# Where operand tiles begin: w and o tiles at 128 mod 256 bytes, the other operand tiles at 0

## The chip, the cores and the metric

The kernel runs on one core of a Trainium2 chip. The metric is the device time of one execution in microseconds; the time before is the median of three runs. One further execution was recorded by the hardware profiler, and every row shown below comes from it.

## The reference: attention, a squared-ReLU MLP and four experts

```python
scores = q @ k.T / sqrt(64)            # 2 x 8 heads, 576 positions, 64 wide
attn = softmax(where(mask, scores, -1e9)) @ v   # heads 0-3: last 32 positions; 4-7: every 32nd
x = attn as (1152, 512)
x = relu(x @ w_in) ** 2 @ w_out        # w_in 512 x 2048, w_out 2048 x 512
p = domain_probs / (domain_probs.sum(-1) + 1e-9)
out = sum over e in 0..3 of p[:, e] * (relu(x @ w1[e]) @ w2[e])   # w1 512 x 1024, w2 1024 x 512
```

All of it is float32.

## The kernel before

A product in the MLP and the experts is made of three matmuls in TensorE's type fp32r. Each operand is kept as two halves, a rounded one ("hi") and what is left ("lo"), and `mm3` (L787 to L790) multiplies hi by hi, hi by lo and lo by hi into one PSUM tile. A matmul has a stationary operand (`lhsT`, 128 columns, brought in by a weight load that the trace shows as a row of its own, PEld) and a moving operand (`rhs`, 384 or 512 columns that stream past it).

Which tile is which operand:

- `x0` to `x2` (the activations, transposed, 384 tokens each), `h0` to `h3` (hidden values) and `t0` to `t2` (sums of activations for the fast matrix products of Strassen's kind) are moving operands of `mm3`. In the second product of an expert, in `second` (L1328 to L1330), hidden values in `h`, `x` or `t` tiles are the stationary operand.
- `w0` to `w9` hold weights that were split into hi and lo, the stationary operand of `mm3`. In the last stage some of them serve otherwise: the first 6144 bytes of such a tile hold sums of activations (moving) and the last 2048 bytes a left operand (stationary). The first two of the second expert weights (`std_w2`) also stand in a w tile, as the moving operand of L1328 to L1330.
- `o0` to `o2` hold all the other second expert weights, split, as the moving operand of L1328 to L1330.
- `q`, `k`, `v`, `p`, `pt` are the attention's, in plain float32; `raw`, `mid`, `val`, `r`, `sf`, `c0`, `acc`, `y0`, `y1` are read and written by DMAs, VectorE, ScalarE and GpSimd only.

The order of the work is written by a planner (`Plan`): every task has a cost, a rank and the tasks it comes after, and a simulation of engines and buffers fixes the order in which instructions are issued. It knows names, costs and free buffers, and no addresses. Attention runs in the first 90 us beside the first MLP products; the MLP follows, then the experts. While TensorE has nothing at the start, a filler (L1477) multiplies the bf16 tile `idle`.

Tiles are laid into SBUF in the order in which they are allocated, pool after pool: `const`, `main`, then `attn` and later `late` in the same place; `early` and later `last` stand at the other end and end at the same byte. The lines that matter:

```python
pe_s = const.tile([P, NT // P], F32, name="pe_s")
xt = many(main, "x", NB, [P, 2, KD, TB], F32R)
...
plan.ring("w", many(main, "w", NW, [P, 2, 4 * CH], F32R))
plan.ring("raw", many(main, "raw", NRAW, [P, 4 * CH], U32))
...
late["w2", k] = rp.tile([P, 2, DM], F32R, name=f"o{k}")
```

In the built program of before `x0` begins at byte 18336 of each partition, 160 mod 256, and since the tiles after it are multiples of 512 bytes long, `w`, `raw`, `mid`, `val`, `h`, `r`, `acc`, `t` and `sf` tiles begin at 160 mod 256 too. The `o` tiles begin at 217056, 221152 and 225248, which is 224 mod 256. The bf16 tile `idle` begins at 17856, 192 mod 256. Every operand of an fp32r matmul is a slice that begins a whole multiple of 512 bytes after its tile.

Of the kernel before, what the change touches and what calls it, by code (L numbers as in the profile page):

```python
# [7 lines left out]
F32 = mybir.dt.float32  # L8
# [8 lines left out]
P = 128  # L17
# [180 lines left out]
def tile_attention_mlp_experts(ctx: ExitStack, tc: tile.TileContext, a, out):  # L198
# [5 lines left out]
    const = ctx.enter_context(tc.tile_pool(name="const", bufs=1))  # L204
    main = ctx.enter_context(tc.tile_pool(name="main", bufs=1))
# [13 lines left out]
    def many(pool, name, n, shape, dtype=F32):  # L219
        return [pool.tile(shape, dtype, name=f"{name}{i}") for i in range(n)]  # L220
# [57 lines left out]
    idle = const.tile([P, P], BF16, name="idle")  # L278
    pe = const.tile([P, NT // P, E], F32, name="pe")
    pe_s = const.tile([P, NT // P], F32, name="pe_s")  # L280
    xt = many(main, "x", NB, [P, 2, KD, TB], F32R)
    spill = many(ep, "y", NB - 1, [P, KD, TB])
    plan.ring("w", many(main, "w", NW, [P, 2, 4 * CH], F32R))
    plan.ring("raw", many(main, "raw", NRAW, [P, 4 * CH], U32))
    plan.ring("mid", many(main, "mid", NMID, [P, 2 * CH]))
    plan.ring("val", many(main, "val", NMID, [P, 2 * CH]))
# [894 lines left out]
    def open_last(e):  # L1181
        early.close()
        rp = ctx.enter_context(tc.tile_pool(name="last", bufs=1, side="right"))
        for k in range(3):
            late["w2", k] = rp.tile([P, 2, DM], F32R, name=f"o{k}")

    t_last = plan.add({"none": 1}, open_last, after=t_sums, rank=0, adds=[("w2", [("w2", k) for k in range(3)]), ("tmp", [("tmp", 0)])])
    plan.add({"none": 1}, lambda e: None, after=[pair_end, t_late], rank=0, adds=[("hid", [("h", k) for k in range(hk)])])

# [377 lines left out]
```

## Time and profile before

| | |
|---|---|
| time, median of 3 runs | 615.72 us (615.61 to 615.83) |
| profiled execution, span from the first to the last instruction | 614.7 us |
| around the span (median less span) | 1.0 us |
| TensorE busy | 608.4 us, 99% of the span |
| VectorE, ScalarE, GpSimd busy | 452.9, 302.4, 125.4 us |
| moved by DMA | 45.14 MB |

Busy shares are of the span. A matmul's record reaches from its start to the modelled end of its drain, so that records of neighbouring matmuls overlap; what a matmul costs is the time from its start to the start of the next one. A row of the timeline that merges several instructions says how many (x6) and reaches from the start of the first to the end of the last.

### The profile page before, as it was taken

Reading aid. Unit: us, or ns where it says so; the run is one execution under the profiler, and the core shown is the slowest. Engines: PE = TensorE matmul, PEld = TensorE weight load, DVE = VectorE, ACT = ScalarE, POOL = GpSimd, SP = SyncE. Lnnn points to the kernel's source line nnn. Section 1 sums busy time; section 2 is a strip of 40 time slices with the busy share of each in tenths; the row PEclk is TensorE's granted clock in tenths of the full one; section 3 lists DMA queues with packets and bytes.
Section 4 is the critical chain, followed back from the end, with each engine's and each line's share of the span. In section 5 each row is a group of like instructions: output and inputs, shape, how many; then the busy total and the mean of one; then the engine's idle time right before and its main releaser. Section 6 shows DMA issues by size and latency. Waiting matters only on the chain.

```text
span 614.7 us, 10054 instructions
## 1 busy us (share of the span) xinstructions
PE 608.4 (99%) x3737; PEld 558.4 (91%) x3737; DVE 452.9 (74%) x900; ACT 302.4 (49%) x705; POOL 125.4 (20%) x150
## 2 busy tenths in 40 slices
PE   8999999999999999999999999999999999999997
PEld 5898999999999999998898989898998989898996
DVE  5997958774797984977666675858866776987654
ACT  3676875656464653665244534344344534344330
POOL 2421202310010101032031231312141322224000
PEclk9999999999999999999999999999999999999999
DMA  8987332131213100020110202020201203020012
GB/s 262 315 262 204 110 110 92 34 108 66 102 50 89 36 0 18 1 86 18 38 49 20 84 18 86 18 86 17 71 16 36 70 17 86 18 86 1 1 52 103
DMA packets 37441, 45.14 MB, mean 73 GB/s; under 512 B 4688, under 2 KB 26640, under 8 KB 37392
## 3 DMA queue, kind: packets, MB, share of 16 engines
q1 hardware_dynamic: 37392, 44.50, 23.7%
q8 instruction: 29, 0.48, 0.3%
q14 instruction: 20, 0.16, 0.1%
HBM read 42.13 MB, written 2.36 MB: 72 GB/s over the span
## 4 chain that ended last, share of the span: by engine, by line
PE 97%; DMA 1%; ACT 0%; DVE 0%; SPq 0%; issue 0%; POOL 0%; ACTq 0%
PE bh L788 12%; PE bh L790 12%; PE bh L789 12%; PE by L1329 11%; PE by L1328 11%; PE by L1330 11%; PE by L788 5%; PE by L790 5%; PE by L789 5%; PE ba L788 4%; PE ba L790 4%; PE ba L789 3%; PE ba L516 1%; PE ba L502 1%; DMA q<-in_ql_dram 1%; DMA k<-in_ks_dram 1%
## 5 line engine op out<-in xcount | busy, mean ns | idle before, releaser
L1281 DVE SCALAR_TENSOR_TENSOR acc<-by,pe,acc 128x512 f32<-128x512 f32 (+1 forms) x109 | 79.3, 743 | 24.2 <-PE by L1330 23.9
L788 PE MATMUL bh<-x,w 128*128 128x384 f32 x234 | 80.4, 344 | 0.0
L790 PE MATMUL bh<-x,w 128*128 128x384 f32 x234 | 78.4, 335 | 0.0
L789 PE MATMUL bh<-x,w 128*128 128x384 f32 x234 | 78.4, 335 | 0.0
L1226 POOL TENSOR_TENSOR sf<-raw,raw 128x256 f32<-128x256 f32 x40 | 32.1, 812 | 185.8 <-DMA raw<-in_w_dram 95.9
L1237 ACT ACTIVATE w<-sf 128x256 fp32r<-128x256 f32 x110 | 42.0, 406 | 35.8 <-POOL sf L1226 35.8
L1329 PE MATMUL by<-o,h 128*128 128x512 f32 (+1 forms) x134 | 52.3, 390 | 0.0
L1328 PE MATMUL by<-o,h 128*128 128x512 f32 (+1 forms) x134 | 52.0, 388 | 0.0
L788 PE MATMUL by<-h,w 128*128 128x384 f32 x152 | 51.8, 341 | 0.0
L1330 PE MATMUL by<-o,h 128*128 128x512 f32 (+1 forms) x134 | 51.7, 386 | 0.0
L790 PE MATMUL by<-h,w 128*128 128x384 f32 x152 | 50.8, 334 | 0.0
L789 PE MATMUL by<-h,w 128*128 128x384 f32 x152 | 50.8, 334 | 0.0
L788 PEld LDWEIGHTS bh<-x,w 128*128 128x128 f32 x234 | 43.9, 188 | 2.5 <-DVE r L1448 1.1
L789 PEld LDWEIGHTS bh<-x,w 128*128 128x128 f32 x234 | 44.0, 188 | 0.4
L790 PEld LDWEIGHTS bh<-x,w 128*128 128x128 f32 x234 | 43.9, 188 | 0.0
L1350 ACT ACTIVATE h<-r 128x384 fp32r<-128x384 f32 x26 | 13.7, 525 | 53.6 <-DVE r L1448 53.6
L1226 POOL TENSOR_TENSOR sf<-sf,raw 128x256 f32<-128x256 f32 x40 | 32.2, 815 | 29.1 <-DVE w L1245 29.0
L1448 DVE TENSOR_TENSOR r<-r,bh 128x384 f32<-128x384 f32 x50 | 27.6, 551 | 12.9 <-ACT r L1443 8.3
L789 PE MATMUL bh<-w,w 128*128 128x384 f32 x110 | 36.9, 336 | 0.0
L790 PE MATMUL bh<-w,w 128*128 128x384 f32 x110 | 36.9, 335 | 0.0
L788 PE MATMUL bh<-w,w 128*128 128x384 f32 x110 | 36.8, 335 | 0.0
L1258 ACT ACTIVATE o<-raw 128x512 fp32r<-128x512 f32 x30 | 18.8, 631 | 35.5 <-PE by L1330 35.1
(286 smaller groups left out, 1607.7 us busy)
## 6 DMA issues: line engine op xcount, KB each, us to landing
raw<-in_wi_dram SPq DMA_DIRECT2D x16, 512.0 KB, 3.5
raw<-in_wo_dram SPq DMA_DIRECT2D x16, 512.0 KB, 3.9
raw<-in_w_dram SPq DMA_DIRECT2D x64, 128.0 KB, 2.7
raw<-in_w_dram SPq DMA_DIRECT2D x32, 256.0 KB, 2.8
out_dram<-acc SPq DMA_DIRECT2D x8, 256.0 KB, 2.0
v<-in_vs_dram SPq DMA_DIRECT2D x6, 256.0 KB, 5.1
v<-in_vl_dram SPq DMA_DIRECT2D x8, 192.0 KB, 5.4
k<-in_kl_dram SPq DMA_DIRECT2D x8, 160.0 KB, 4.9
```

What stands on the lines that cost most here:

```text
L788: nc.tensor.matmul(dst, lhsT=wh, rhs=xh, start=start, stop=False, skip_group_check=again)
L789: nc.tensor.matmul(dst, lhsT=wh, rhs=xl, start=False, stop=False, skip_group_check=again)
L790: nc.tensor.matmul(dst, lhsT=wl, rhs=xh, start=False, stop=stop, skip_group_check=again)
L1226: nc.gpsimd.tensor_tensor(out=value(dst), in0=value(x), in1=value(y), op=ALU.subtract if n in MINUS else ALU.add)
L1237: nc.scalar.activation(out=op_slot(env["op"])[:, 0].rearrange("p k f -> p (k f)"), in_=value(src), func=AF.Copy, scale=float(sign))
L1258: nc.scalar.activation(out=late[env["w2"]][:, 0], in_=f32(raws[f]["raw"][:, DM:]), func=AF.Copy)
L1281: nc.vector.scalar_tensor_tensor(out=acc, in0=o, scalar=pcol, in1=acc, op0=ALU.mult, op1=ALU.add)
L1328: nc.tensor.matmul(o, lhsT=h[:, 0, ts], rhs=w[:, 0], start=new, stop=False)
L1329: nc.tensor.matmul(o, lhsT=h[:, 0, ts], rhs=w[:, 1], start=False, stop=False)
L1330: nc.tensor.matmul(o, lhsT=h[:, 1, ts], rhs=w[:, 0], start=False, stop=stop)
L1350: nc.scalar.activation(out=got(env["hid"])[:, 0], in_=src(), func=AF.Relu)
L1448: nc.vector.tensor_tensor(out=at_(), in0=at_(), in1=bank["bank"][:, :TB], op=ALU.add if sign > 0 else ALU.subtract)
```

## The change

It allocates four tiles that no instruction reads or writes, so that the tiles behind them begin elsewhere.

```diff
     pe_s = const.tile([P, NT // P], F32, name="pe_s")
+    const.tile([P, 24], F32, name="gap0")
     xt = many(main, "x", NB, [P, 2, KD, TB], F32R)
     spill = many(ep, "y", NB - 1, [P, KD, TB])
+    main.tile([P, 32], F32, name="gap2")
     plan.ring("w", many(main, "w", NW, [P, 2, 4 * CH], F32R))
+    main.tile([P, 32], F32, name="gap3")
     plan.ring("raw", many(main, "raw", NRAW, [P, 4 * CH], U32))
...
         for k in range(3):
             late["w2", k] = rp.tile([P, 2, DM], F32R, name=f"o{k}")
+        rp.tile([P, 24], F32, name="gap1")
```

`gap0` is 96 bytes: `x0` moves from 18336 to 18432 = 72 x 256. `gap2` is 128 bytes: `w0` moves from 55200 to 55424, which is 128 mod 256. `gap3`, again 128 bytes, brings `raw` and everything behind it to 0 mod 256 (352 bytes further than before). `gap1` makes the pool `last` 96 bytes longer; it ends where it ended, so the o tiles begin 96 bytes earlier, at 216960, 128 mod 256. `y0`, `y1` and the tiles of `const` before `gap0` stay.

## Rows read from the trace of the kernel before

**Rows 1.** The page: busy time of each engine, TensorE's granted clock by slice.
```profile
span 614.7 us, 10054 instructions
PE 608.4 (99%) x3737; PEld 558.4 (91%) x3737; DVE 452.9 (74%) x900; ACT 302.4 (49%) x705; POOL 125.4 (20%) x150
...
PEclk9999999999999999999999999999999999999999
```

**Rows 2.** The page, the chain that ended last, by engine and line.
```profile
PE 97%; DMA 1%; ACT 0%; DVE 0%; SPq 0%; issue 0%; POOL 0%; ACTq 0%
PE bh L788 12%; PE bh L790 12%; PE bh L789 12%; PE by L1329 11%; PE by L1328 11%; PE by L1330 11%; PE by L788 5%; PE by L790 5%; PE by L789 5%; PE ba L788 4%; PE ba L790 4%; PE ba L789 3%; PE ba L516 1%; PE ba L502 1%; DMA q<-in_ql_dram 1%; DMA k<-in_ks_dram 1%
```

**Rows 3.** By stage: us, PE, PEld, DVE, ACT, POOL busy; clock, DMA share, GB/s.
```profile
20.00:40.00 20.00, 19.71 (x275) 16.70 (x271) 19.47 (x52) 13.90 (x42) 6.55 (x7) 1.00 1.02 319
...
120.00:140.00 20.00, 20.00 (x117) 20.00 (x116) 13.15 (x24) 11.68 (x23) 3.10 (x3) 1.00 0.33 105
...
420.00:440.00 20.00, 20.00 (x96) 17.35 (x95) 19.56 (x40) 7.74 (x20) 5.87 (x7) 1.00 0.05 14
```

**Rows 4.** Timeline in the MLP: start us, us, engine, line, operation, tiles, shape.
```profile
119.92 0.33 PE L788 MATMUL bh<-x,w 128*128 128x384 f32 x1
119.92 0.19 PEld L789 LDWEIGHTS bh<-x,w 128*128 128x128 f32 x1
...
120.96 0.33 PE L788 MATMUL by<-h,w 128*128 128x384 f32 x1
```

**Rows 5.** Timeline, expert output from a w tile; what follows nine matmuls later.
```profile
253.22 0.39 PE L1328 MATMUL by<-w,t 128*128 128x512 f32 x1
...
255.26 0.33 PE L788 MATMUL ba<-x,w 128*128 128x384 f32 x1
```

**Rows 6.** Timeline, expert output from o tiles: first and sixteenth matmul.
```profile
300.19 0.39 PE L1328 MATMUL by<-o,h 128*128 128x512 f32 x1
...
303.62 0.39 PE L1328 MATMUL by<-o,h 128*128 128x512 f32 x1
```

**Rows 7.** Timeline, the bf16 filler: runs of six, of one and of two.
```profile
9.43 1.47 PE L1477 MATMUL by<-idle 128*128 128x512 bf16 x6
...
21.50 0.38 PE L1477 MATMUL by<-idle 128*128 128x512 bf16 x1
...
21.50 0.59 PE L1477 MATMUL by<-idle 128*128 128x512 bf16 x2
```

**Rows 8.** Attention scores in float32: timeline, and the group with its mean.
```profile
60.96 1.54 PE L502 MATMUL ba<-k,q 64*64 64x96 f32 x32
...
L502 PE MATMUL ba<-k,q 64*64 64x96 f32 x128 | 7.0, 248 | 0.5 <-DMA q<-in_ql_dram 0.4 <-DVE p L554 0.2
```

**Rows 9.** Counts of L788 and L1328, and of groups that move w.
```profile
0.00:615.00 615.00, 237.69 (x700) 131.37 (x700) 1.00 0.24 73
...
0.00:615.00 615.00, 113.26 (x291) 54.63 (x291) 1.00 0.24 73
...
L788 PE MATMUL bh<-w,w 128*128 128x384 f32 x110 | 36.8, 335 | 0.0
...
L788 PE MATMUL ba<-w,w 128*128 128x384 f32 x36 | 12.1, 336 | 0.0
...
L788 PE MATMUL bh<-w 128*128 128x384 f32 x10 | 3.3, 335 | 0.0
...
L788 PE MATMUL ba<-w 128*128 128x384 f32 x4 | 1.3, 336 | 0.0
...
L1328 PE MATMUL by<-w,h 128*128 128x512 f32 x12 | 4.7, 389 | 0.0
...
L1328 PE MATMUL by<-w,t 128*128 128x512 f32 x6 | 2.3, 389 | 0.0
```

**Rows 10.** The chain in time, its first two transfers: start us, us.
```profile
2.12 4.48 DMA k<-in_ks_dram
...
6.61 4.70 DMA q<-in_ql_dram
```

## The prediction

> **What bounds the kernel now.** I read the page first: TensorE is busy 608.4 of 614.7 us and its granted clock is at its upper level, 2.4 GHz, in every slice [rows 1]. The chain of waits agrees: 97% of it is TensorE, and its longest shares are the matmuls of mm3 (L788 to L790) and of the second experts (L1328 to L1330) [rows 2]. The table by stage shows who else is near its limit: from 20 to 40 us VectorE (19.47 of 20) and the DMA engines (1.02); in some later stretches VectorE again (19.56 from 420 us); in a stretch like 120 to 140 us VectorE has 6.9 us to spare and the others more [rows 3]. So time comes or goes by what one matmul takes from its start to the start of the next, and a busy share doesn't show that, since matmuls overlap. The timeline does. Every third matmul of mm3 is an L788, and six matmuls take 120.96 - 119.92 = 1.04 us: 0.52 from one L788 to the next, 173.3 ns for a matmul of 384 columns. The weight load of the next one starts with it and takes 0.19 us, so a load always lies beside the moving stream [rows 4]. A column a cycle at 2.4 GHz would be 160.0 ns: 13.3 ns are extra. With 512 columns and the moving operand in a w tile it is (255.26 - 253.22) / 9 = 226.7 ns, again 13.3 over 213.3 [rows 5]; with an o tile it is (303.62 - 300.19) / 15 = 228.7 ns, 15.4 over [rows 6]. The bf16 filler, 512 columns with a weight load before each, takes (1.47 - 0.38) / 5 = 0.218 us in a run of six and 0.59 - 0.38 = 0.21 in a run of two (0.38 is a single one to its end): some 216 ns, 2.7 over [rows 7].
>
> **The change part by part.** It adds four tiles that nobody reads or writes. No instruction, wait, DMA or order is added, removed or moved: the planner works with costs and names, not addresses. What changes is where tiles begin. Before, x, w, h and T tiles all begin at 160 mod 256 and the o tiles at 224. Slices of these tiles are whole multiples of 512 bytes, so in every pair of matmul and next weight load the two operands stand 0 apart (mod 256) where w meets x, h or T, and 64 apart where o meets them. After: x, h and T (and raw, mid, val, acc) at 0, w and o at 128. Three prices follow.
>
> (1) Pairs that go from distance 0 to 128. L788 runs 700 times, of which 110 + 36 + 10 + 4 = 160 have both operands in w tiles and stay at distance 0 [rows 9]: 540 x 3 = 1620 matmuls of 384 columns. Of the 291 of L1328, 12 + 6 take w as the moving operand [rows 9]: 54 of 512 columns.
> (2) The others, 273 x 3 = 819 with an o tile, go from 64 to 128.
> (3) Everything else only begins at a multiple of 64 bytes where it was 32 beside one: VectorE, ScalarE and GpSimd on their tiles, and the landings of the DMAs. I price it at nothing. The engines are covered by TensorE, which is busy throughout in the later stretches of [rows 3]; without the cover a change of a few per cent in VectorE would count in the two full stretches alone, less than 1 us. The DMAs that count are the first two in the chain, 4.48 and 4.70 us [rows 10]; a tenth of them, either way, is 0.9 us.
>
> What (1) and (2) cost a matmul no row shows, since no fp32r pair of before is 128 apart. Bounds: the most that can come back is what lies over the filler, 13.3 - 2.7 = 10.6 ns for (1) and 12.7 for (2): 1674 x 10.6 + 819 x 12.7 = 17.7 + 10.4 = 28 us. The nearest row for the size of an address effect is the 2.0 ns between [rows 5] and [rows 6]: same columns, same weights, 64 bytes of distance. One such step is the low end, two (128 bytes) the high end; I take one and a half, 3.0 ns below the level at distance 0, as a gain. The reason for the sign: the 13.3 ns are the same for 384 and 512 columns, so they belong to something that happens once a matmul, as the load of 128 weights does; the filler with half the bytes in both streams nearly lacks them; and the attention matmuls in plain fp32, whose columns pass at half the rate, lack them too: 32 in 1.54 us, less the last one's 0.25, are 81 ns a pair (the two halves of the array run side by side, and each matmul of the code stands twice in the trace), where two passes over 96 columns make 80 [rows 8]. It looks like two streams of full rate that get into each other's way, and now both begin on the same low address bits. The reason is weak: 64 bytes of distance made it worse, not better.
> Sum: 1674 x 3.0 = 5.0 us; for (2) from 228.7 to 223.7, 819 x 5.0 = 4.1 us; together 9.1. Before 40 us VectorE and the DMAs set the pace; I take off 0.6 for it. 615.7 - 8.5 = 607.2, against the profiled execution's own 614.7 and the 1.0 around it, which is the median of the runs, 615.72.
>
> A rule of the Trainium skill (TensorE: Matmul & The Clock Gate, "Wait — 56ns, not 53.3ns?") says that at full clock matmuls start N/2.4 plus about 2.5 ns apart. The filler agrees with its 216 ns; the fp32r matmuls with 13.3 and 15.4 do not. If the change brought all but the w,w pairs to that rule, the sum would be 1674 x 10.8 + 819 x 12.9 = 28.6 us and the time 587, an estimate from that page.
>
> **Rivals.** *No change.* The extra time is a fixed part of an fp32r matmul with its weight load, whatever the addresses. For it: 0.52 us for three stands in [rows 4] and, with 117 matmuls in or reaching into 20 us, in the row of 120 to 140 us in [rows 3], over tiles in quite different places; and in [rows 8] the distance of keys and queries alternates between 0 and 128 (the second half t of the keys begins 160 columns, 640 bytes, after the first, the queries' 256 bytes), and the pair takes its 81 ns on the mean, next to the 80 of its columns. Against it: the 2.0 ns between [rows 5] and [rows 6]. Time 615.7, and 614 if only o falls back to the 226.7 of [rows 5] (819 x 2.0 = 1.6 us). The Trainium skill (SBUF — State Buffer, "Who interferes with whom") speaks for this rival: TensorE has two independent read ports there, one for the moving operand and one for weights, and never waits for anyone. The trace agrees as far as rows 4 go and not in the 2.0 ns; by the rule the time stays 615.7.
>
> *Slower.* The distance of 64 cost 2.0 ns; if 128 costs twice that, every pair of (1) rises to 177.3 ns and o to 230.7: 1674 x 4.0 + 819 x 2.0 = 8.3 us, 624.0; with one step, 1674 x 2.0 and nothing for o, 619.0. It decides as soon as (1) loses more than 0.7 ns a matmul, 1.2 us in all. For it: the only comparison in the trace has this sign. Against it: distance 0 need not be the best, since its 13.3 ns are five times the filler's.
>
> *Full relief.* All that lies over the filler goes: 615.7 - 28 = 587.7, less if VectorE then sets the pace in its full stretches (0.44 us of spare in 20 against 1.2 of gain, [rows 3]); some 589. For it: the same 13.3 ns at both lengths, as if one cause made all of it.
>
> **How the numbers follow.** Partial relief 0.45, its own range 597 to 614; full relief 0.10; no change 0.20; slower 0.25, from 617 to 626. The forecast is the first, 607. To hold 8 in 10 the range runs from 587, the end of full relief, to 621, which leaves out about half of the slower case and some of full relief. A difference under 0.2% (1.2 us) can't be told from none here. Faster takes partial and full relief, 0.55; same 0.20; slower 0.25.
>
> **What the profile after would show.** Right: L788 to L788 outside w,w pairs at 0.51 us for three, where it was 0.52; in [rows 6] 0.67 for three where it was 0.686; 118 to 119 matmuls from 120 to 140 us where it was 117; w,w pairs still at 0.52. Full relief: 0.49 and 0.65. No change: the same to the hundredth. Slower: 0.53 and more. I am wrong in the step itself if x/w pairs stand and only o moves, or if w,w pairs, whose distance doesn't change, move as much as the others: then it is where a tile begins that counts, not the distance between two. And if VectorE or DMA durations move by more than a few per cent, price (3) was wrong.

## The result: slower by 0.9%

The changed kernel took 621.59 us (621.50 to 621.71), the kernel before, measured beside it, 615.78 us. The ratio is 1.0088, with a 95% interval of 1.0077 to 1.0100: 5.8 us slower, where 607.0 was forecast, and 0.6 us beyond the upper end of the range. Its profiled execution has a span of 619.7 us, 5.0 longer than before.

First the page of the kernel after, for [rows 1] and [rows 2]: busy times, granted clock, and the chain that ended last. The change moved the code by three or four lines: L788 to L790 are now L791 to L793, L1328 to L1330 are L1332 to L1334.

```profile
span 619.7 us, 10054 instructions
PE 613.6 (99%) x3737; PEld 561.8 (91%) x3737; DVE 454.0 (73%) x900; ACT 302.9 (49%) x705; POOL 124.1 (20%) x150
...
PEclk9999999999999999999999999999999999999999
...
PE 97%; DMA 1%; SPq 0%; ACT 0%; DVE 0%; issue 0%; POOL 0%; ACTq 0%
PE bh L791 12%; PE bh L793 12%; PE bh L792 12%; PE by L1333 11%; PE by L1334 11%; PE by L1332 11%; PE by L791 5%; PE by L793 5%; PE by L792 5%; PE ba L791 3%; PE ba L793 3%; PE ba L792 3%; PE ba L519 1%; PE ba L505 1%; DMA q<-in_qs_dram 1%; PE ba L433 1%
```

The clock is granted in every slice as before, the chain has the same make-up, and the count of instructions is the same. PE's busy time grew by 5.2 us, VectorE's by 1.1 and ScalarE's by 0.5; GpSimd's fell by 1.3. So the time is lost in TensorE's own stream. Two of the stretches of [rows 3], same columns:

```profile
20.00:40.00 20.00, 20.00 (x268) 17.06 (x269) 19.46 (x52) 13.96 (x39) 6.08 (x6) 1.00 0.96 312
120.00:140.00 20.00, 20.00 (x116) 20.00 (x115) 12.86 (x24) 11.73 (x24) 3.16 (x3) 1.00 0.31 103
```

From 120 to 140 us 116 matmuls fit where 117 did; the forecast wanted 118 to 119. The timeline of the kernel after says what one takes. First the six matmuls of [rows 4], then the nine of [rows 5] and the 24 of mm3 that follow them, then the fifteen of [rows 6]:

```profile
120.05 0.34 PE L791 MATMUL bh<-x,w 128*128 128x384 f32 x1
...
121.10 0.34 PE L791 MATMUL by<-h,w 128*128 128x384 f32 x1
...
254.87 0.39 PE L1332 MATMUL by<-w,t 128*128 128x512 f32 x1
...
256.95 0.34 PE L791 MATMUL ba<-x,w 128*128 128x384 f32 x1
...
261.16 0.39 PE L1332 MATMUL by<-w,t 128*128 128x512 f32 x1
...
301.00 0.40 PE L1332 MATMUL by<-o,h 128*128 128x512 f32 x1
...
304.51 0.39 PE L1332 MATMUL by<-o,h 128*128 128x512 f32 x1
```

Six of mm3 take 1.05 us, 175.0 ns each (173.3 before). Nine with a w tile as the moving operand take 2.08 us, 231.1 ns (226.7). Fifteen with an o tile take 3.51 us, 234.0 ns (228.7). The 24 of mm3 take 4.21 us, 175.4 ns; in the kernel before the same 24 run from the 255.26 of [rows 5] to this row of its timeline, 4.18 us or 174.2 ns:

```profile
259.44 0.39 PE L1328 MATMUL by<-w,t 128*128 128x512 f32 x1
```

A hundredth of a microsecond is coarse for such differences, so I took every pair of consecutive fp32r matmuls from the starts in both traces, sorted by the tiles of the moving operand and of the next weight load. The distance is the moving operand's begin less that of the stationary one, mod 256. For 384 columns the mean leaves out pairs with a wait (200 ns and more); these sum to 11.0 us before and 10.7 after, in the 1585.

```
columns, moving, next load   pairs   distance    ns before   ns after   sum of all
384   x/h/t, w               1585    0 -> 128      173.79     175.92      +3.1 us
384   w, w                    460    0 -> 0        174.13     174.18       0.0 us
512   o, x/h/t                772    64 -> 128     229.35     232.30      +2.3 us
512   o, w                     29    64 -> 0       225.83     233.69      +0.2 us
512   w, x/h/t                 52    0 -> 128      228.23     232.79      +0.2 us
```

The sum, before rounding, is 5.9 us (51 pairs of other kinds change by 0.01 us), beside 5.8 us by the medians: the loss lies in these pairs. The spans of the two recorded executions differ by 5.1 us alone, since the one after began its first fp32r matmul earlier, at 21.15 us instead of 21.75. No run puts that down to the change: this begin is at 21.77 us in `o160` and 21.22 in `all0` below, whose medians are 0.3 us apart, and at 23.14 in `w192_o0`, the fastest of all by its median. In four of the rows a matmul's own weights stand at the distance of the next load; in the row "o, w", the last o matmul of a group, they stand at 64 before and 128 after, and the loss of one pair, 7.9 ns, is the largest of all. The w,w pairs stand still, as the prediction had it for pairs whose distance does not change.

The other engines did not stand still. Six of VectorE's sums into t tiles, before and after (line, operation, tiles, busy us, mean ns, idle before it):

```profile
L1009 DVE TENSOR_TENSOR t<-acc,t 128x384 fp32r<-128x384 f32 x6 | 4.7, 801 | 0.0
```
```profile
L1012 DVE TENSOR_TENSOR t<-acc,t 128x384 fp32r<-128x384 f32 x6 | 5.6, 942 | 0.0
```

One of the six takes 1.40 us where it took 0.55. The begin of its tiles is not the cause: in `w96_o0` below, acc and t stand at the same bytes as here and the mean is 802. From rows not shown: the 30 instructions that split into o tiles went from 707 to 688 ns, 26 that make h tiles from r from 585 to 612, while the two largest groups stand at 742 ns beside 743 and at 429 beside 424. What made these move no run shows. In time nothing of it can be seen, since the fp32r pairs hold the whole loss and the h group takes even more, 654 ns, in `all0`, which is no slower than before. All DMA bytes are the same 45.14 MB; the median landing of the four large transfers from `in_ks` went from 5.0 to 4.5 us, and it is 4.3 in `o160`, where their tiles stand as before, so that such a difference is no sign of the change.

### The profile page after: what moved, and what is told of

It is laid out like the page before. It is cut to its first block, busy times and chain, and to the rows that moved or that the text cites. A ratio compares the mean times of both kernels' runs of the same rounds, so it can differ in the third digit from the quotient of the medians.

```text
span 619.7 us, 10054 instructions
## 1 busy us (share of the span) xinstructions
PE 613.6 (99%) x3737; PEld 561.8 (91%) x3737; DVE 454.0 (73%) x900; ACT 302.9 (49%) x705; POOL 124.1 (20%) x150
## 2 busy tenths in 40 slices
DMA packets 37441, 45.14 MB, mean 73 GB/s; under 512 B 4688, under 2 KB 26640, under 8 KB 37392
## 4 chain that ended last, share of the span: by engine, by line
PE 97%; DMA 1%; SPq 0%; ACT 0%; DVE 0%; issue 0%; POOL 0%; ACTq 0%
PE bh L791 12%; PE bh L793 12%; PE bh L792 12%; PE by L1333 11%; PE by L1334 11%; PE by L1332 11%; PE by L791 5%; PE by L793 5%; PE by L792 5%; PE ba L791 3%; PE ba L793 3%; PE ba L792 3%; PE ba L519 1%; PE ba L505 1%; DMA q<-in_qs_dram 1%; PE ba L433 1%
## 5 line engine op out<-in xcount | busy, mean ns | idle before, releaser
L791 PE MATMUL bh<-x,w 128*128 128x384 f32 x234 | 81.1, 346 | 0.0
L793 PE MATMUL bh<-x,w 128*128 128x384 f32 x234 | 79.1, 338 | 0.0
L1334 PE MATMUL by<-o,h 128*128 128x512 f32 (+1 forms) x134 | 52.4, 391 | 0.0
L791 PE MATMUL by<-h,w 128*128 128x384 f32 x152 | 52.4, 345 | 0.0
L1332 PE MATMUL by<-o,h 128*128 128x512 f32 (+1 forms) x134 | 52.3, 390 | 0.0
L793 PE MATMUL by<-h,w 128*128 128x384 f32 x152 | 51.4, 338 | 0.0
L792 PE MATMUL by<-h,w 128*128 128x384 f32 x152 | 51.3, 337 | 0.0
L791 PEld LDWEIGHTS bh<-x,w 128*128 128x128 f32 x234 | 43.9, 188 | 2.4 <-DVE r L1452 1.1
L793 PEld LDWEIGHTS bh<-x,w 128*128 128x128 f32 x234 | 43.9, 188 | 0.0
L791 PE MATMUL bh<-w,w 128*128 128x384 f32 x110 | 37.0, 336 | 0.0
L793 PE MATMUL bh<-w,w 128*128 128x384 f32 x110 | 36.9, 336 | 0.0
```

The costliest lines, as they stand in the source:

```text
L791: nc.tensor.matmul(dst, lhsT=wh, rhs=xh, start=start, stop=False, skip_group_check=again)
L792: nc.tensor.matmul(dst, lhsT=wh, rhs=xl, start=False, stop=False, skip_group_check=again)
L793: nc.tensor.matmul(dst, lhsT=wl, rhs=xh, start=False, stop=stop, skip_group_check=again)
L1332: nc.tensor.matmul(o, lhsT=h[:, 0, ts], rhs=w[:, 0], start=new, stop=False)
L1334: nc.tensor.matmul(o, lhsT=h[:, 1, ts], rhs=w[:, 0], start=False, stop=stop)
```

## Experiments

The theories. *Distance*: what a pair of matmul and weight load costs depends on the distance of their operands mod 256, and 0 is good. *Absolute begin*: it depends on where the tiles themselves begin, and the change put them in a bad place. On the 13.3 ns over a column a cycle, *weight load*: they come from the load that runs beside the stream, as the prediction had it; *every matmul*: they stay whatever the load does, so nothing was there to win. Where an expectation uses letters, D is the distance, A the absolute begin, N a reason other than the address, L the weight load and F the part that every fp32r matmul has.

### One part of the move at a time

`o160` and `all0` put all operands at distance 0, one at the 160 of before, the other at 0:

```diff
# o160: o tiles from 224 to 160, all else as before
         for k in range(3):
             late["w2", k] = rp.tile([P, 2, DM], F32R, name=f"o{k}")
+        rp.tile([P, 16], F32, name="gap1")
# all0: every operand tile at 0
+    const.tile([P, 24], F32, name="gap0")
...
+        rp.tile([P, 56], F32, name="gap1")
```

> The kernel before with one pad of 64 bytes behind the o tiles, so that they begin at 160 mod 256 like all others: every pair of moving operand and next weight load stands 0 apart. Theory D, that the distance between the two counts: the 512-column matmuls with an o tile fall from 229.3 ns to the 226.7 of those with a w tile, 801 x 2.6 = 2.1 us, about 613.7. Theory A, that only where a tile begins counts (160, 224, 0, 128): o at 160 becomes what w at 160 was, the same 613.7, so this run alone does not part them. Theory N, that o is slower for another reason than its address: 615.8.

> The changed kernel without its shift of w and o: x, w, h, T and o tiles all begin at 0 mod 256. Theory D (distance): all pairs 0 apart, 384 columns at 173.3 ns, 512 columns at 226.7, about 613.7, as in the run with all at 160. Theory A (begin of a tile): x, h and T begin at 0 as in the changed kernel, whose 384-column pairs of x, h or T with w took 175.9, so these stay at 175.9 and the time is near 619; w,w pairs may move too.

`w128_o64` makes the step (1) of the prediction alone, `w0_o128` the step (2) alone:

```diff
# w128_o64: x, h, t at 0, w at 128, o 64 from its stationary operand, as before
+    const.tile([P, 24], F32, name="gap0")
+    main.tile([P, 32], F32, name="gap2")
+    main.tile([P, 32], F32, name="gap3")
...
+        rp.tile([P, 40], F32, name="gap1")
# w0_o128: x, h, t and w at 0, o at 128
+    const.tile([P, 24], F32, name="gap0")
...
+        rp.tile([P, 24], F32, name="gap1")
```

> The changed kernel with the o tiles at 64 mod 256 instead of 128, as far from h, x and T as they were before; w stays 128 away from x, h and T. Theory D: the 384-column pairs of x, h or T with w keep their 175.9 ns (3.1 us above before), the o matmuls go back to 229.3, together about 619.1. Theory A: o at 64 is a new place, x and w are as in the changed kernel; anything from 619 to 622. If the o tiles made the whole loss, 616.

> The other part of the change alone: x, w, h and T tiles at 0 mod 256, o tiles at 128. Theory D (distance): the 384-column pairs stay at 173.8 ns, the o matmuls take the 232.3 of the changed kernel in place of the 228.3 of the run with all at 0: 801 x 4.0 = 3.2 us above its 615.1, 618.4. If the two parts share a cause that needs both, it is less than 617.

Measured, each beside runs of the kernel before (615.78 to 616.06 us), with the pair means from its trace:

```
kernel     x/h/t to w, o to h   us       ratio [95%]               384 x/h/t,w   512 o,x/h/t   512 w,x/h/t
before          0,  64           -         -                          173.79        229.35        228.23
after         128, 128         621.59   1.0088 [1.0077, 1.0100]       175.92        232.30        232.79
o160            0,   0         615.40   0.9987 [0.9979, 0.9996]       173.80        228.28        228.25
all0            0,   0         615.14   0.9987 [0.9978, 0.9996]       173.80        228.28        228.23
w128_o64      128,  64         619.09   1.0053 [1.0039, 1.0067]       175.89        229.72        232.48
w0_o128         0, 128         618.73   1.0042 [1.0030, 1.0055]       173.68        233.28        228.23
```

o160 and all0 agree to the hundredth of a nanosecond in the large classes, with x and w 96 bytes apart: the absolute begin falls. Both gained 0.8 us where 2.1 were expected: the 226.7 ns of [rows 5] is one stretch of nine, and the o pairs fell to 228.3, the mean of the pairs with a moving operand in w. Each part costs alone what the table above gives it, 0.53% and 0.42%, about 3.3 and 2.6 us, together 5.9 beside the 5.8 of the whole change. The o matmuls of `w0_o128` (first fence) and `w128_o64` (second), the same fifteen as above, in the timeline:

```profile
298.29 0.40 PE L1330 MATMUL by<-o,h 128*128 128x512 f32 x1
...
301.80 0.39 PE L1330 MATMUL by<-o,h 128*128 128x512 f32 x1
```
```profile
300.81 0.39 PE L1332 MATMUL by<-o,h 128*128 128x512 f32 x1
...
304.25 0.39 PE L1332 MATMUL by<-o,h 128*128 128x512 f32 x1
```

3.51 us at distance 128, 234.0 ns each as in the kernel after; 3.44 us, 229.3 ns, at 64. The begin of the w tiles, 0 in `w0_o128` and 128 in the kernel after, does not show in these fifteen; over all such pairs the means are 233.3 and 232.3 ns.

### Runs of matmuls by themselves

`streams` leaves the whole computation of the reference out. It runs 37 sets of fp32r matmuls after a warm-up, one after another on the same operands, 36 in each set, and changes only where the two operands begin:

```diff
+    for k in range(36):  # columns 384, s 0, m 128
+        nc.tensor.matmul(b[0][:, :384], lhsT=s_at(0), rhs=m_at(128, 384), start=k == 0, stop=k == 35)
```

> A kernel of its own that leaves the whole computation out: runs of 36 fp32r matmuls, each with its weight load, from one weight tile and one moving tile, and only the first bytes of the two operands change from run to run (distance 0 to 256 in steps of 16 with 384 columns, of 32 with 512, four places of the weights, 256 columns, and 2048 bytes further). Theory D: 173.3 ns at distance 0 and more at 128 with 384 columns, 226.7 and about 232 with 512, the same at distance 256 and 2048 as at 0, and the same for all four places of the weights. Theory A: the four places of the weights differ from each other at the same distance. If neither counts in a pure stream, all runs of one length are alike to 1 ns.

Its timeline: a row is one set, and the time from its start to the next row's start, over 36, is the time of a matmul. L42 to L64 are 384 columns at distances 0, 16, 32 and so on; L76 to L90 are 512 columns in steps of 32; L92 to L106 are 384 columns with the weights at 32, 64, 128 and 160, each at distance 0 and then 128.

```profile
19.37 6.43 PE L42 MATMUL b<-mv,wt 128*128 128x384 f32 x36
25.63 6.47 PE L44 MATMUL b<-mv,wt 128*128 128x384 f32 x36
...
56.98 6.52 PE L54 MATMUL b<-mv,wt 128*128 128x384 f32 x36
63.34 6.40 PE L56 MATMUL b<-mv,wt 128*128 128x384 f32 x36
69.58 6.50 PE L58 MATMUL b<-mv,wt 128*128 128x384 f32 x36
75.91 6.45 PE L60 MATMUL b<-mv,wt 128*128 128x384 f32 x36
82.19 6.52 PE L62 MATMUL b<-mv,wt 128*128 128x384 f32 x36
88.55 6.50 PE L64 MATMUL b<-mv,wt 128*128 128x384 f32 x36
...
126.57 8.36 PE L76 MATMUL b<-mv,wt 128*128 128x512 f32 x36
134.77 8.57 PE L78 MATMUL b<-mv,wt 128*128 128x512 f32 x36
143.18 8.41 PE L80 MATMUL b<-mv,wt 128*128 128x512 f32 x36
151.43 8.57 PE L82 MATMUL b<-mv,wt 128*128 128x512 f32 x36
159.84 8.56 PE L84 MATMUL b<-mv,wt 128*128 128x512 f32 x36
168.24 8.59 PE L86 MATMUL b<-mv,wt 128*128 128x512 f32 x36
```

384 columns: 6.26 us at distance 0, 173.9 ns, and 6.33 at 128 (L58), 175.8 ns; 6.24 at 112 (173.3), 6.36 at 96 and 160 (176.7). 512 columns: 8.20 at 0 (227.8), 8.25 at 64 (229.2), 8.40 at 128 (233.3). These are close to the kernel's numbers, with nothing else running. The first matmuls of a set that follows one of another length are uneven (171 to 185 ns in L42, 224 to 236 in L76), which makes the 173.9 and the 227.8; later ones in these two sets take 173 or 174 and 226 or 227. By the same rule from rows not shown: four places of the weights give 173.3 to 174.2 at distance 0 and 175.8 to 176.1 at 128, and 2048 bytes more give 173.3 as well. So for operands that stay in their places it is the distance mod 256. It is not a smooth function of it: 240 gives 179.7, 256 again 173.3. And no set of 384 or 512 columns goes below 173.3 and 226.7: distance 0 already stands within about 1 ns of the best that was found.

### Two more distances in the kernel

`w192_o0` and `w96_o0` keep o at 0 from h and put x, h and t 64 and 160 from the weights:

```diff
# w192_o0; w96_o0 has 24 in gap2 and 40 in gap3, else the same
+    const.tile([P, 24], F32, name="gap0")
+    main.tile([P, 48], F32, name="gap2")
+    main.tile([P, 16], F32, name="gap3")
...
+        rp.tile([P, 56], F32, name="gap1")
```

> As all at 0 mod 256, but w at 192: a moving operand in x, h or T begins 64 bytes after the weights, a distance at which the stream of 384 columns took 173.2 ns. If the pure streams carry over to the kernel: 384-column pairs near 173.5, the 54 matmuls from a w tile at the stream's 233.3 of distance 192 (+0.3 us), 615.3 in all, as good as distance 0. If the kernel only knows distance 0 as good: the 175.9 of distance 128, 618.5.

> As all at 0 mod 256, but w at 96: x, h and T begin 160 bytes after the weights, where the stream of 384 columns took 176.7 ns. If the pure streams carry over: 1585 x 3.0 = 4.8 us, with the 54 matmuls from w at 233.4 0.3 more, 620.2, worse than distance 128. If what counts is only whether the distance is 0, as with distance 128: 618.3.

`w192_o0` took 614.62 us, ratio 0.9979 [0.9970, 0.9988]; its x/h/t,w pairs take 173.29 ns and its o pairs 227.47. It is the best of all layouts tried, 0.2% ahead of the kernel before; it ran on another chip than all0, and their intervals overlap. Its recorded execution was the slowest of its eleven, 616.46 us, with a weight transfer of 7.84 us in its chain at the start; its fp32r pairs sum to 1.1 us less than before. Its w,w pairs, still at distance 0, rose to 175.27 ns, and no theory here explains that, nor why w,w pairs take 174.22 ns in `all0` and 173.47 in `w0_o128`, where the o tiles alone stand elsewhere.

`w96_o0` missed what the stream had promised, and the 618.3 of the other theory too: 615.82 us, 0.9992 [0.9980, 1.0004], with 174.11 ns for the x/h/t,w pairs where the stream had 176.7 at a distance of 160. The timeline shows two kinds of stretches, six matmuls of mm3 and the 24 beside [rows 5]:

```profile
118.00 0.34 PE L791 MATMUL bh<-x,w 128*128 128x384 f32 x1
...
119.04 0.34 PE L791 MATMUL bh<-x,w 128*128 128x384 f32 x1
...
254.66 0.34 PE L791 MATMUL ba<-x,w 128*128 128x384 f32 x1
...
258.90 0.40 PE L1332 MATMUL by<-w,t 128*128 128x512 f32 x1
```

1.04 us for six are 173.3 ns; 4.24 us for 24 are 176.7. At this distance the cost depends on something else as well.

### Is it the weight load?

`streams2`, again without the reference's computation, shortens the weight load (128, 96, 64, 32 columns) and takes other lengths and bf16:

```diff
+    for k in range(36):  # fp32r, columns 384, weight columns 32, distance 0
+        nc.tensor.matmul(b[0][:32, :384], lhsT=s_at(0, 32), rhs=m_at(0, 384), start=k == 0, stop=k == 35)
```

> Again a kernel of its own that leaves the whole computation out: runs of 36 matmuls with 128, 96, 64 and 32 columns of weights to load, 384 and 512 moving columns, distance 0 and 128; other lengths of the moving operand; distances of 4 and 8 bytes; and bf16. Theory L, that the extra time is the weight load beside the moving stream: it shrinks with the columns that are loaded, from 13.3 ns at 128 to about 3 at 32 (if only the slower distance is the load's, then 2.7 and 6.7 ns go to nothing and 13.3 stays). Theory F, a fixed part of every fp32r matmul: 13.3 ns at all four widths. bf16 stays near 2.5 ns over its columns at both distances under both theories, as its halved bytes leave room.

In its timeline L46 to L60 are 384 columns with 128, 96, 64 and 32 weight columns, each at distance 0 and then 128; L108 and L110 are bf16 at the same two distances:

```profile
21.70 6.43 PE L46 MATMUL b<-mv,wt 128*128 128x384 f32 x36
27.97 6.50 PE L48 MATMUL b<-mv,wt 128*128 128x384 f32 x36
34.30 6.46 PE L50 MATMUL b<-mv,wt 128*96 128x384 f32 x36
40.60 6.41 PE L52 MATMUL b<-mv,wt 128*96 128x384 f32 x36
46.85 6.41 PE L54 MATMUL b<-mv,wt 128*64 128x384 f32 x36
...
59.33 6.40 PE L58 MATMUL b<-mv,wt 128*32 128x384 f32 x36
65.57 6.40 PE L60 MATMUL b<-mv,wt 128*32 128x384 f32 x36
71.81 8.37 PE L62 MATMUL b<-mv,wt 128*128 128x512 f32 x36
...
232.85 6.02 PE L108 MATMUL b<-mb,wb 128*128 128x384 bf16 x36
238.71 6.01 PE L110 MATMUL b<-mb,wb 128*128 128x384 bf16 x36
244.56 7.93 PE L112 MATMUL b<-mb,wb 128*128 128x512 bf16 x36
```

With 32 weight columns a load's own record falls from 188 to 108 ns, and the matmul keeps its 6.24 us in 36, 173.3 ns. So the 13.3 ns do not shrink with the columns that are loaded, and the theory of the weight load falls in that form. A fixed cost of a load is not excluded, as every matmul here has one. The extra at distance 128 does hang on the load: 6.33 us with 128 weight columns, 6.25 (173.6 ns) with 96 and 6.24 with 32. But with 96 columns distance 0 is the slower one, 6.30 us or 175.0 ns. With 512 columns the picture is mixed: 228.1 and 233.1 ns at the two distances with 128 weight columns, 231.4 and 230.6 with 32. bf16 takes 162.8 and 162.5 ns at 384 columns, whatever the distance.

The Trainium skill (TensorE: Matmul & The Clock Gate, "Wait — 56ns, not 53.3ns?") puts warm matmuls N/2.4 plus about 2.5 ns apart; bf16 agrees with its 2.5 over 160.0 here, and no fp32r set of 384 or 512 columns comes within 10 ns of it.

### Whose load, and operands that change place

`streams3`, also without the computation, lets the operands alternate between two places, and repeats the kernel's own order of slices (high, high, low weights; high, low, high activations):

```diff
+    for k in range(36):  # columns 384, 0 from its own load, 128 from the next
+        nc.tensor.matmul(b[1][:, :384], lhsT=s_at(128 * (k % 2)), rhs=m_at(128 * (k % 2), 384), start=k == 0, stop=k == 35)
+    for k in range(36):  # columns 384, as mm3, distance 160
+        nc.tensor.matmul(b[1][:, :384], lhsT=s_at(mm3_s(k)), rhs=m_at(mm3_m(k) + 160, 384), start=k == 0, stop=k == 35)
```

> Runs of 36 fp32r matmuls each, nothing else of the computation (all of the reference's work is left out). Question one: to which weight load does the distance belong, to a matmul's own or to the one that is loaded beside it? With 384 columns, two places in turn. Own load: 0 from its own and 128 from the next stays at 173.3 ns, 128 from its own and 0 from the next gives 176.0. Next load: the other way round, 176.0 and 173.3. Both count: something between or above for each. With weights or moving operand alone in turn, half of the pairs stand 128 apart by either theory: 174.7 on the mean. With 512 columns the same with 226.7 and 233.3. Question two: why did a distance of 160 cost 3.4 ns in the pure stream and only 0.3 ns in the kernel? If the operands that change place from matmul to matmul (weight slices high, high, low; activations high, low, high) make the difference, the run as in mm3 gives 173.3 to 174 at distances 0, 64, 160 and 192, and 175.9 at 128; if not, 176.7 at 160, and what the kernel showed has another cause. As in the second experts, 512 columns: 228.3 at 0, 229.4 at 64, 233 at 128 and, as the pure stream had it, 233.3 at 192.

In its timeline L55 has all at 0; L57 is 0 from its own load and 128 from the next, L59 the reverse; L79 to L83 are as in mm3 at 128, 160 and 192:

```profile
20.24 6.43 PE L55 MATMUL b<-mv,wt 128*128 128x384 f32 x36
26.50 6.47 PE L57 MATMUL b<-mv,wt 128*128 128x384 f32 x36
32.81 6.50 PE L59 MATMUL b<-mv,wt 128*128 128x384 f32 x36
39.16 6.48 PE L61 MATMUL b<-mv,wt 128*128 128x384 f32 x36
...
105.60 6.49 PE L79 MATMUL b<-mv,wt 128*128 128x384 f32 x36
111.93 6.42 PE L81 MATMUL b<-mv,wt 128*128 128x384 f32 x36
118.18 6.45 PE L83 MATMUL b<-mv,wt 128*128 128x384 f32 x36
124.47 8.32 PE L85 MATMUL b<-mv,wt 128*128 128x512 f32 x36
```

173.9 ns with all at 0 (173 or 174 after its first matmuls, which are uneven again), 175.3 with only the next load 128 away, 176.4 with only the own one: both count, and neither of the two simple theories holds. With the kernel's order of places, 128 gives 175.8 as before, and 160 falls from 176.7 to 173.6: places that change from matmul to matmul take away most of the cost of 160, as in the mean of `w96_o0`; why its stretch of 24 still pays 176.7 is not shown. At 192 it gives 174.7. As in the second experts, by the same rule from rows not shown: 226.7 at 0, 229.4 at 64 and 232.2 at 128. One operand alone in turn between 0 and 128 gives 175.6 (weights) and 175.0 (moving) at 384 columns. The kernel's classes of 512 columns agree within 1.6 ns (228.3 at 0, 229.4 at 64, 232.3 to 233.3 at 128).

## Why the prediction was wrong

**What was right.** That only the start-to-start time of fp32r matmuls could move the kernel; which pairs change their distance, and about how many; that w,w pairs stay; price (3), nothing for all other work. VectorE's durations did move by more than a few per cent in small groups, from 801 to 942 ns in one, which the prediction had named as a sign against (3); the price held even so, since the fp32r pairs hold the whole loss. The rival *Slower* names the mechanism that happened: distance 128 costs more than 0 and more than 64.

**The step that failed** is the sign in (1) and (2): "I take one and a half, 3.0 ns below the level at distance 0, as a gain". Measured was a loss of 2.1 ns in the 384-column pairs, 4.6 in the few with w moving, and 3.0 in the o pairs, where a gain of 5.0 was forecast. With the prediction's own counts that is 1620 x 2.1 + 54 x 4.6 + 819 x 3.0 = 3.4 + 0.2 + 2.5 = 6.1 us where the traces show 5.9 and the runs 5.8; the prediction had -9.1.

**Why it failed.** The sign hung on the thought that the 13.3 ns over a column a cycle were two streams in each other's way. `streams2` shows that at 384 columns they stay with a quarter of the load, and the streams show nothing under 173.3 and 226.7 ns at any distance tried: from the means of before down to these levels, 1585 x 0.5 + 460 x 0.8 + 772 x 2.6 ns = 3.2 us was the most that a layout could give, by the distances tried, and `w192_o0` got 1.3 of it; the 28 us that the prediction let come back at most were not there. The prediction noted that "the only comparison in the trace has this sign", the 2.0 ns between [rows 5] and [rows 6], and set it aside for an argument from the size of the extra time, of which no row shows a gain by a distance. all0 and o160 confirm its sign: 0.9987, the 0.8 us that 772 pairs gain with 1.1 ns each. The size of the step, 2.0 ns, came from two short stretches and was nearly twice that.

**The size.** *Slower* spanned 619.0 (one step, nothing for o) to 624.0 (two steps, +4.0 and +2.0). The truth lies between: one step for (1), 2.1 ns, and more than that for o, 3.0. A count of steps by bytes was the wrong scale for both, since the streams show no steady slope. The upper end of 621 cut off half of a rival that had the trace's one comparison on its side.

**What stays open.** Why 128 costs 2.1 to 2.7 ns at 384 columns and 4 to 5.5 at 512, and why the dependence on distance is so uneven (173.3 at 112, 176.7 at 96 and 160), was not settled. The runs show that the own and the next load both count, that 64 or 32 weight columns remove it at 384 columns (with 96 the order turns round) but not clearly at 512, and that the order of places decides at 160. The Trainium skill (SBUF — State Buffer, "Who interferes with whom") gives TensorE two independent read ports and says that it waits for no one; these runs, with 175.8 against 173.9 ns and no other engine at work, are hard to fit to that for fp32r, though no run shows that the time is lost in reading.

## What to carry to other kernels

When a kernel is bound by one engine's back-to-back stream, one per cent can hang on where its operands begin (614.62 to 621.59 us here), and neither a busy share nor a chain of waits shows it; only start to start does. If a trace holds one comparison of the effect in question, take its sign before any argument about causes; and before pricing what might come back, ask whether the present state is already the best one, which a short run of the operation alone answers. For fp32r matmuls here: keep the moving operand and the weights at distance 0 or, at 384 columns, the moving operand 64 bytes (mod 256) after the weights, and avoid 128.

## What the runs showed of the hardware

- An fp32r matmul of 384 or 512 columns takes 13.3 ns more than a column a cycle at its best (173.3 and 226.7 ns), and at 384 columns keeps them when the weight load shrinks from 128 to 32; bf16 takes 2.5 more (162.5). 256 columns take 120.0 and 119.7 ns at distance 0 in `streams` and `streams2`; at 64 they take 113.6 in the one and 117.8 in the other, a difference that is not explained. A column a cycle would be 106.7.
- The distance of the two operands mod 256 bytes moves this by up to 6.4 ns at 384 columns (179.7 at 240) and 7.5 at 512 (234.2 at 160); at a distance of 4 bytes it is 178.6 and 236.7 ns. The absolute place does not count at the distances 0 and 128 in the places tried, and the order in which operands change their places does (176.7 against 173.6 ns at a distance of 160).
